# Local attention in 32-query chunks with four heads in 128 rows, value products in four array tiles, and new planner constants, in an attention and expert-MLP kernel on one core

## The chip, the core and the metric

The kernel runs on one core of a Trainium2 chip. The time is device microseconds of one execution, and the comparison uses the median of several runs. The core's engines work in parallel and wait for each other on semaphores: TensorE (PE; its weight loads appear apart, as PEld), VectorE (DVE), ScalarE (ACT), GpSimd (POOL), and SyncE (SP), whose queue issues the transfers from and to device memory.

## What is computed

```python
def _attn_ref(q, k, v):                       # B, H, S, D = 2, 8, 576, 64
    scores = (1 / np.sqrt(D)) * np.matmul(q, k.transpose(0, 1, 3, 2))
    rel = pos[:, None] - pos[None, :]
    mask_local = (rel >= 0) & (rel < 32)                              # heads 0 to 3
    mask_strided = (rel >= 0) & (pos[None, :] % 32 == pos[:, None] % 32)   # heads 4 to 7
    ...                                       # masked softmax
    return np.matmul(attn, v)

def reference(...):
    x = attention laid out as (B * S, H * D)  # 1152 tokens, 512 wide
    x = relu(x @ w_in) ** 2 @ w_out           # d_ff = 2048
    out = sum over e of p[:, e] * (relu(x @ w1[e]) @ w2[e])           # 4 experts, 1024 wide
```

## The kernel before

**Three stages.** Attention is done first and partly beside the first MLP; then come the first MLP and the experts. Every MLP product is three PE products (`mm3`, L788 to L790, and L1328 to L1330 in the experts): operands are split into a high and a low part of a short float32 format, and high by high, high by low and low by high are added up in one PSUM bank.

**The order.** `Plan` (L69) is a small scheduler that runs while the program is built. Each task names the engines that may run it, its cost, a rank, what it comes after, and the buffers that it takes and frees. Whenever an engine is free in the plan, it gets the ready task of the lowest rank. The program is then written out in the plan's order, so each engine's order is fixed by costs and ranks, and a table of constants (L222 to L274) sets the ranks. Where PE has nothing to do in the plan ahead of the first MLP product, `plan.filler` puts a 512-column product on zeros there (L1477).

**A set of attention** (`attend`, L525) goes through these steps: load keys, queries and values; `scores` on PE into a bank S; on DVE the maximum and the subtraction, on ACT the exponential, on DVE the sum and its reciprocal, on POOL or DVE the normalisation; `transposes` on PE into a bank T; a copy to `pt` on ACT or DVE; `values` on PE into a bank X; then the high part and the low part of the result into `xt`, the first MLP's input. A set either gets its mask on PE (a product of the identity with the mask, L426 or L497) or on DVE (L554). With `whole` the exponential is one ACT instruction and the sum one on DVE; without it ACT does one exponential with an accumulated sum per unit (L566).

**Strided sets** (L389) hold 2 or 3 residues of the 32 times 18 positions: 36 or 54 queries by as many keys, 8 units, two heads in the two halves of the 128 rows. There are three sets for each of the two batches. Their 16 value products (L447) go to two tiles of the array, since rows and columns both follow `k`:

```python
nc.tensor.matmul(env["X"][k * D : (k + 1) * D, c : c + n], lhsT=env["v3"][rows, 2 * g + h, :], ...)
```

**Local sets** (L460) hold 128 queries (two of the ten hold 64) in chunks of `WQ` = 64 queries by `WIN` = 96 keys. A unit is one chunk of two heads, one in each half of the 128 rows; a set of 128 queries has 4 units, 8 score products of 64 x 96 (L502), 4 transposes (L506) and 8 value products with 96 rows of keys (L516).

Six sets start before the first MLP product (three strided, three local, `startup`, L601), seven run beside the first steps of the MLP and three beside the next ones. The MLP's first steps read only the first block of 384 tokens.

**Profile names.** `by`, `bh` and `ba` are PSUM banks (four, two and two), `idle` the zeros of the filler, `cb` the constants, `w` split weights, `raw` loaded ones.

## Time and profile before

| | before |
|---|---|
| median of 3 runs | 616.07 us (615.63 to 616.36) |
| span of the profiled execution | 614.7 us |
| PE busy | 608.4 us, 99% of the span, 3737 products |
| DVE busy | 452.9 us, 74% |
| ACT busy | 302.4 us, 49% |
| POOL busy | 125.4 us, 20% |
| read from device memory | 42.13 MB |

The span runs from the first to the last instruction that the profiler recorded; a run's time has some 1.4 us around it. Busy is the union of an engine's rows, and a PE row is longer than the time until the next product starts, because products are pipelined. So PE is read from start to start.

### The profile page before, as it was taken

To read this page: it belongs to the slowest core of one execution; us is meant where nothing else is said; L and a number is where in the kernel's file an instruction comes from. 1 tells how busy PE (TensorE), PEld (TensorE's weight loads), DVE (VectorE), ACT (ScalarE), POOL (GpSimd) and SP (SyncE) were. 2 spreads that over 40 slices of the span, in tenths; PEclk is the share of its full clock that TensorE was granted. 3 is DMA by queue.
4 is the path that set the end of the run, shared out by engine and by line. 5 is a ranking of instruction groups with operands and counts; after the bars stand their busy time and mean duration, and the time that the engine had idled before them with its cause. 6 is when DMAs were issued, how large, how long until landed. Compare 5 with 4: busy or idle time off the path is not lost.

```text
span 614.7 us, 10054 instructions
## 1 busy us (share of the span) xinstructions
PE 608.4 (99%) x3737; PEld 558.4 (91%) x3737; DVE 452.9 (74%) x900; ACT 302.4 (49%) x705; POOL 125.4 (20%) x150
## 2 busy tenths in 40 slices
PE   8999999999999999999999999999999999999997
PEld 5898999999999999998898989898998989898996
DVE  5997958774797984977666675858866776987654
ACT  3676875656464653665244534344344534344330
POOL 2421202310010101032031231312141322224000
PEclk9999999999999999999999999999999999999999
DMA  8987332131213100020110202020201203020012
GB/s 262 315 262 204 110 110 92 34 108 66 102 50 89 36 0 18 1 86 18 38 49 20 84 18 86 18 86 17 71 16 36 70 17 86 18 86 1 1 52 103
DMA packets 37441, 45.14 MB, mean 73 GB/s; under 512 B 4688, under 2 KB 26640, under 8 KB 37392
## 3 DMA queue, kind: packets, MB, share of 16 engines
q1 hardware_dynamic: 37392, 44.50, 23.7%
q8 instruction: 29, 0.48, 0.3%
q14 instruction: 20, 0.16, 0.1%
HBM read 42.13 MB, written 2.36 MB: 72 GB/s over the span
## 4 chain that ended last, share of the span: by engine, by line
PE 97%; DMA 1%; ACT 0%; DVE 0%; SPq 0%; issue 0%; POOL 0%; ACTq 0%
PE bh L788 12%; PE bh L790 12%; PE bh L789 12%; PE by L1329 11%; PE by L1328 11%; PE by L1330 11%; PE by L788 5%; PE by L790 5%; PE by L789 5%; PE ba L788 4%; PE ba L790 4%; PE ba L789 3%; PE ba L516 1%; PE ba L502 1%; DMA q<-in_ql_dram 1%; DMA k<-in_ks_dram 1%
## 5 line engine op out<-in xcount | busy, mean ns | idle before, releaser
L1281 DVE SCALAR_TENSOR_TENSOR acc<-by,pe,acc 128x512 f32<-128x512 f32 (+1 forms) x109 | 79.3, 743 | 24.2 <-PE by L1330 23.9
L788 PE MATMUL bh<-x,w 128*128 128x384 f32 x234 | 80.4, 344 | 0.0
L790 PE MATMUL bh<-x,w 128*128 128x384 f32 x234 | 78.4, 335 | 0.0
L789 PE MATMUL bh<-x,w 128*128 128x384 f32 x234 | 78.4, 335 | 0.0
L1226 POOL TENSOR_TENSOR sf<-raw,raw 128x256 f32<-128x256 f32 x40 | 32.1, 812 | 185.8 <-DMA raw<-in_w_dram 95.9
L1237 ACT ACTIVATE w<-sf 128x256 fp32r<-128x256 f32 x110 | 42.0, 406 | 35.8 <-POOL sf L1226 35.8
L1329 PE MATMUL by<-o,h 128*128 128x512 f32 (+1 forms) x134 | 52.3, 390 | 0.0
L1328 PE MATMUL by<-o,h 128*128 128x512 f32 (+1 forms) x134 | 52.0, 388 | 0.0
L788 PE MATMUL by<-h,w 128*128 128x384 f32 x152 | 51.8, 341 | 0.0
L1330 PE MATMUL by<-o,h 128*128 128x512 f32 (+1 forms) x134 | 51.7, 386 | 0.0
L790 PE MATMUL by<-h,w 128*128 128x384 f32 x152 | 50.8, 334 | 0.0
L789 PE MATMUL by<-h,w 128*128 128x384 f32 x152 | 50.8, 334 | 0.0
L788 PEld LDWEIGHTS bh<-x,w 128*128 128x128 f32 x234 | 43.9, 188 | 2.5 <-DVE r L1448 1.1
L789 PEld LDWEIGHTS bh<-x,w 128*128 128x128 f32 x234 | 44.0, 188 | 0.4
L790 PEld LDWEIGHTS bh<-x,w 128*128 128x128 f32 x234 | 43.9, 188 | 0.0
L1350 ACT ACTIVATE h<-r 128x384 fp32r<-128x384 f32 x26 | 13.7, 525 | 53.6 <-DVE r L1448 53.6
L1226 POOL TENSOR_TENSOR sf<-sf,raw 128x256 f32<-128x256 f32 x40 | 32.2, 815 | 29.1 <-DVE w L1245 29.0
L1448 DVE TENSOR_TENSOR r<-r,bh 128x384 f32<-128x384 f32 x50 | 27.6, 551 | 12.9 <-ACT r L1443 8.3
L789 PE MATMUL bh<-w,w 128*128 128x384 f32 x110 | 36.9, 336 | 0.0
L790 PE MATMUL bh<-w,w 128*128 128x384 f32 x110 | 36.9, 335 | 0.0
L788 PE MATMUL bh<-w,w 128*128 128x384 f32 x110 | 36.8, 335 | 0.0
L1258 ACT ACTIVATE o<-raw 128x512 fp32r<-128x512 f32 x30 | 18.8, 631 | 35.5 <-PE by L1330 35.1
(286 smaller groups left out, 1607.7 us busy)
## 6 DMA issues: line engine op xcount, KB each, us to landing
raw<-in_wi_dram SPq DMA_DIRECT2D x16, 512.0 KB, 3.5
raw<-in_wo_dram SPq DMA_DIRECT2D x16, 512.0 KB, 3.9
raw<-in_w_dram SPq DMA_DIRECT2D x64, 128.0 KB, 2.7
raw<-in_w_dram SPq DMA_DIRECT2D x32, 256.0 KB, 2.8
out_dram<-acc SPq DMA_DIRECT2D x8, 256.0 KB, 2.0
v<-in_vs_dram SPq DMA_DIRECT2D x6, 256.0 KB, 5.1
v<-in_vl_dram SPq DMA_DIRECT2D x8, 192.0 KB, 5.4
k<-in_kl_dram SPq DMA_DIRECT2D x8, 160.0 KB, 4.9
```

The costliest lines, as they stand in the source:

```text
L788: nc.tensor.matmul(dst, lhsT=wh, rhs=xh, start=start, stop=False, skip_group_check=again)
L789: nc.tensor.matmul(dst, lhsT=wh, rhs=xl, start=False, stop=False, skip_group_check=again)
L790: nc.tensor.matmul(dst, lhsT=wl, rhs=xh, start=False, stop=stop, skip_group_check=again)
L1226: nc.gpsimd.tensor_tensor(out=value(dst), in0=value(x), in1=value(y), op=ALU.subtract if n in MINUS else ALU.add)
L1237: nc.scalar.activation(out=op_slot(env["op"])[:, 0].rearrange("p k f -> p (k f)"), in_=value(src), func=AF.Copy, scale=float(sign))
L1258: nc.scalar.activation(out=late[env["w2"]][:, 0], in_=f32(raws[f]["raw"][:, DM:]), func=AF.Copy)
L1281: nc.vector.scalar_tensor_tensor(out=acc, in0=o, scalar=pcol, in1=acc, op0=ALU.mult, op1=ALU.add)
L1328: nc.tensor.matmul(o, lhsT=h[:, 0, ts], rhs=w[:, 0], start=new, stop=False)
L1329: nc.tensor.matmul(o, lhsT=h[:, 0, ts], rhs=w[:, 1], start=False, stop=False)
L1330: nc.tensor.matmul(o, lhsT=h[:, 1, ts], rhs=w[:, 0], start=False, stop=stop)
L1350: nc.scalar.activation(out=got(env["hid"])[:, 0], in_=src(), func=AF.Relu)
L1448: nc.vector.tensor_tensor(out=at_(), in0=at_(), in1=bank["bank"][:, :TB], op=ALU.add if sign > 0 else ALU.subtract)
```

## The change

**Local sets.** A set is now 192 queries in six chunks of 32 queries by 64 keys. A unit is one chunk with all four local heads in the 128 rows, 32 rows each, so a set has 6 units and 24 score products of 32 stationary columns by 64 moving ones, in tiles of 64 rows by 32 columns (two row halves, four column quarters). Two units fill 128 columns of transposed probabilities, so there are 3 transposes. There are 24 value products with 64 rows of keys: the first 64 rows of `pt` belong to the even chunk, the others to the odd one, and each goes to a bank of its own. Six sets take the place of ten.

**Strided value products.** The 16 products are arranged so that four neighbours use the four 64 x 64 tiles of the array: row half `k` and column half `t`. Results of row half 0 go to one bank and those of row half 1 to a second (`env["X", k]`). The score columns are placed so that the transposes deliver this arrangement. The results of every set are read from two banks, in two groups of instructions.

**Loads and constants.** Values are loaded in two transfers per set, one for each half of the rows, without the unused rows; the identity is copied by POOL from `cb` instead of loaded. The planner gets new costs, a cost of 96 ns for changing between tiled and whole-array products, and a new table of ranks, some of which order the weights' conversions and the loads. Five sets come in `startup` (three strided, two local), five in `second`, two in `third`; `ON_PE` and `WHOLE` choose anew which sets are masked on PE and which use one exponential.

```diff
-LOCAL = [[(0, 128), (128, 128), (256, 128), (384, 128), (512, 64)], [(0, 128), (128, 64), (192, 128), (320, 128), (448, 128)]]
-WQ = 64
+NQ_LOCAL = 192
+WQ = 32
 WIN = WQ + STRIDE
...
+    SWITCH = 96
...
-    AHEAD = 10013
-    END2 = 24614
-    END3 = 330
-    CONV = 22941
+    AHEAD = 13732
+    END2 = 22305
+    END3 = 1017
+    CONV = -15359
...
-    CONV1 = 31773
-    CONV2 = -8455
-    FETCH = 252
-    WITH2 = 817
+    CONV1 = -16486
+    CONV2 = -30904
+    FETCH = 40753
+    WITH2 = -2290
...
-    SQ = (0, 23, 0)
-    R_MASK = -916
-    ON_PE = (1, 0, 1, 0, 0, 0, 0, 0, 0, 0)
+    SQ = (0, 23, 1)
+    R_MASK = -2381
+    ON_PE = (1, 1, 0, 0, 0, 0, 0)
...
-    FIRST = (-22394, 16695, 607, 23035, 8563, 1593)
-    WHOLE = (1, 1, 1, 0, 0, 0)
...
+    FIRST = (-13817, -42960, 12541, -38237, -55708)
+    WHOLE = (0, 1, 1, 0, 1, 1, 1, 1, 1, 1, 0, 1)
...
+    LKQ = (-3919, -33009, -13533, -6546, 255)
+    LV = (23587, -34844, 3981, 825, 14657)
+    LW = {('wi', 0, 1): -15243, ('wi', 0, 0): -28071, ('wi', 1, 1): -26551, ('wo', 0, 0): -24768, ('wo', 0, 1): 22478, ('wi', 1, 0): -30156}
+    EARLY = {('wi', 0, 1): 15489, ('wi', 0, 0): -52228, ('wi', 1, 1): 84864, ('wo', 0, 0): -23863, ('wo', 0, 1): -5263, ('wi', 1, 0): -9637}
...
     GROUP = 4
-    AHEAD_H = 3
...
+    AHEAD_H = 1
+    EARLY_H = ((26018, -36435, -4566, -1488), (-17825, 12070, 65861, 27367), (-40517, -11597, 24938, 24933), (66282, -32711, 29856, -6782))
...
-    plan.ring("k", many(at, "k", NQ, [P, U * N3]))
-    plan.ring("v", many(at, "v", NV, [P, 512]))
+    plan.ring("k", many(at, "k", NQ, [P, KCOLS]))
+    plan.ring("v", many(at, "v", NV, [P, VCOLS]))
...
     def mm_r(n):
-        return int(n / 2.4) + 13
+        return 229 if n == 512 else int(n / 2.4) + 13
...
-    t_ci = plan.add({"dma": dma(P * P * 4)}, lambda e: nc.sync.dma_start(out=ident, in_=a["ci"]), rank=L_ID)
+    t_ci = plan.add({"pool": 450}, lambda e: nc.gpsimd.tensor_copy(ident, cb[:, :P]), after=[t_cb], rank=L_ID)
...
-            self.nx = 2 * GROUPS * n
-            self.bytes = [P * U * n * 4, P * U * n * 4, P * U * D * 4]
-            self.cost_s = mm_r(U * n) + 2 * U * packed(n, n) + 100
+            self.nx = GROUPS * n
+            self.bytes = [P * U * n * 4, P * U * n * 4, 2 * n * U * D * 4]
+            self.cost_s = U * (104 if n > 36 else 93)
...
-            self.cost_v = 4 * GROUPS * packed(n, D)
+            self.cost_v = GROUPS * 150
...
-                nc.sync.dma_start(out=env["v"], in_=a["vs"][b, self.j])
+                src = a["vs"][b, self.j].rearrange("(t p) (k c) -> k p t c", t=2, k=2)
+                for k in range(2):
+                    nc.sync.dma_start(out=env["v"][k * D : k * D + n, : U * D].rearrange("p (t c) -> p t c", t=2), in_=src[k, :n])
...
         def values(self, env):
             n = self.n
-            for h in range(2):
-                for g in range(GROUPS):
-                    c, q = (h * GROUPS + g) * n, g * P + h * D
-                    for k in range(2):
-                        rows = slice(k * D, k * D + n)
-                        nc.tensor.matmul(env["X"][k * D : (k + 1) * D, c : c + n], lhsT=env["v3"][rows, 2 * g + h, :], rhs=env["pt"][rows, q : q + n], start=True, stop=True)
...
+            for g in range(2):
+                for h in range(2):
+                    for t in range(2):
+                        c, q = (h * 2 + g) * n, (t * 2 + g) * P + h * D
+                        for k in range(2):
+                            rows = slice(k * D, k * D + n)
+                            nc.tensor.matmul(env["X", k][t * D : (t + 1) * D, c : c + n], lhsT=env["v3"][rows, t, g, h, :], rhs=env["pt"][rows, q : q + n], start=True, stop=True)
...
+        def results(self):
+            parts, m = [], 0
...
+                for x in range(2):
+                    def ends(env, blk=blk, c=c, k=k, m=m, x=x):
+                        src = env["X", x][:, : self.nx].rearrange("p (h r m) -> p h m r", h=2, m=NM)[:, :, m : m + k]
+                        r = self.r0 + 2 * x * self.R
+                        dst = xt[blk][:, :, 2:4, c : c + k * STRIDE].rearrange("p s h (m r) -> p s h m r", r=STRIDE)[:, :, :, :, r : r + 2 * self.R]
+                        return dst, src
...
-            self.t0, self.nq = LOCAL[b][j]
-            self.nj = self.nq // WQ
-            self.units, self.cols, self.pitch = 2 * self.nj, WIN, WIN
-            self.nx = 2 * self.nq
...
+            self.b, self.t0 = b, j * NQ_LOCAL
+            self.nq = NQ_LOCAL
+            self.units, self.cols, self.pitch = self.nq // WQ, WIN, WIN
+            self.nx = self.nq
...
+            self.cost_s = self.units * 120
+            self.pairs = self.units // 2
+            self.cost_t = self.pairs * 109
+            self.cost_v = self.pairs * 180
...
-                nc.sync.dma_start(out=env["v"][:WIN, : 4 * nq], in_=a["vl"][b, :, t0 * 4 : (t0 + nq) * 4])
+                src = a["vl"][b, :, t0 * 8 : (t0 + nq) * 8].rearrange("p (j k c) -> k p j c", k=2, c=4 * D)
+                for k in range(2):
+                    nc.sync.dma_start(out=env["v"][k * D : (k + 1) * D, : 4 * nq].rearrange("p (j c) -> p j c", c=4 * D), in_=src[k])
...
             for u in range(units):
-                j, t = divmod(u, 2)
-                for h in range(2):
-                    hd = slice(h * D, (h + 1) * D)
-                    nc.tensor.matmul(s[hd, u * WIN : (u + 1) * WIN], lhsT=env["q3"][hd, u, :], rhs=env["k3"][hd, t, j * WQ : j * WQ + WIN], start=not masked, stop=not masked or u == units - 1)
+                for t in range(2):
+                    for h in range(2):
+                        hd, r, c = slice(h * D, (h + 1) * D), (2 * h + t) * WQ, u * WIN
+                        nc.tensor.matmul(s[r : r + WQ, c : c + WIN], lhsT=env["q3"][hd, 2 * u + t, :], rhs=env["k3"][hd, t, u * WQ : u * WQ + WIN], start=not masked, stop=not masked or u == units - 1)
...
         def transposes(self, env):
-            for u in range(self.units):
-                nc.tensor.transpose(env["T"][:WIN, u * P : (u + 1) * P], env["p"][:, u * WIN : (u + 1) * WIN], ident)
-
-        def pt_shape(self):
-            return WIN, self.units * P
+            for g in range(self.pairs):
+                cs = slice(g * P, (g + 1) * P)
+                nc.tensor.transpose(env["T"][:, cs], env["p"][:, cs], ident)
...
         def values(self, env):
-            for u in range(self.units):
-                for h in range(2):
-                    j, t = divmod(u, 2)
-                    c = t * self.nq + j * WQ
...
+            for j in range(self.pairs):
+                for t in range(2):
+                    c = (t * self.pairs + j) * WQ
+                    for h in range(2):
+                        for half_ in range(2):
+                            rows, q = slice(half_ * D, (half_ + 1) * D), j * P + (2 * h + t) * WQ
+                            nc.tensor.matmul(env["X", half_][h * D : (h + 1) * D, c : c + WQ], lhsT=env["v3"][rows, j, 2 * t + h, :], rhs=env["pt"][rows, q : q + WQ], start=True, stop=True)
...
-        t = plan.add({"pe": g.cost_t}, lambda e: g.transposes(env), after=[t, t_ci], rank=rank + r_t, take=[(env, "T", rings)], free=[(env, "p")])
+        t = plan.add({"pe": g.cost_t}, lambda e: g.transposes(env), after=[t, t_ci], rank=rank + r_t, take=[(env, "T", rings), (env, "pt", ["pt"])], free=[(env, "p")])
...
-        t_v = plan.add({"pe": g.cost_v}, lambda e: g.values(env), after=[t, loads[2]], rank=rank + r_v, take=[(env, "X", rings)], free=[(env, "pt"), (env, "v")])
+        t_v = plan.add({"pe": g.cost_v}, lambda e: g.values(env), after=[t, loads[2]], rank=rank + r_v, take=[(env, ("X", k), rings) for k in range(2)], free=[(env, "pt"), (env, "v")], tiled=True)
...
-    startup = [Strided(0, j) for j in range(3)] + [Local(0, j) for j in range(3)]
+    startup = [Strided(0, j) for j in range(3)] + [Local(0, j) for j in range(2)]
...
-    second = [Local(0, 3), Local(0, 4)] + [Strided(1, j) for j in range(3)] + [Local(1, 0), Local(1, 1)]
+    second = [Local(0, 2)] + [Strided(1, j) for j in range(3)] + [Local(1, 0)]
     for k, g in enumerate(second):
-        attend(g, START - AHEAD + k * (due(half) - START - END2) // len(second), ["bank_a"], LEAD, whole=g.units > 4, on_pe_=ON_PE[k])
-    third = [Local(1, j) for j in (2, 3, 4)]
+        attend(g, START - AHEAD + k * (due(half) - START - END2) // len(second), ["bank_a"], LEAD, whole=WHOLE[5 + k], on_pe_=ON_PE[k])
+    third = [Local(1, j) for j in (1, 2)]
...
+        attend(g, due(half) - AHEAD + k * (due(2 * half) - due(half) - END3) // len(third), ["bank_a"], LEAD, whole=WHOLE[10 + k], on_pe_=ON_PE[len(second) + k])
```

**Ahead of the first MLP product, on PE.** Here is what stands between two fillers in the middle of the startup, before; `k`, `q` are a set's keys and queries, `p` probabilities, `pt` transposed ones.

```order
L497 LDWEIGHTS cb
L497 MATMUL ba_105<-cb 128x384
L502 MATMUL ba_105<-k_115,q_111 64x96 x8
L447 MATMUL by_108<-pt_130,v_119 64x54 x16
L435 MATMUL ba_106<-ident,p_127 128x128 x4
L497 LDWEIGHTS cb
L497 MATMUL by_109<-cb 128x384
L502 MATMUL by_109<-k_116,q_112 64x96 x8
```

And now, with rows of further products of the same kind left out at the dots:

```order
L444 MATMUL by_107<-cb 128x432
L450 MATMUL by_107<-k_118,q_114 54x54 x16
L465 MATMUL ba_106<-pt_129,v_119 64x54
L465 MATMUL by_108<-pt_129,v_119 64x54
...
L455 MATMUL by_109<-ident,p_125 128x128 x4
L1506 LDWEIGHTS idle
L1506 MATMUL by_110<-idle 128x512
...
L520 LDWEIGHTS cb
L520 MATMUL ba_105<-cb 128x384
L525 MATMUL ba_105<-k_115,q_111 32x64 x24
L530 MATMUL ba_106<-ident,p_126 128x128 x3
```

A value set's products now alternate between two banks; a local set has 24 score products and 3 transposes; the third local score set (`by_109<-k_116`) has moved behind the first MLP products, and fillers stand at places where attention stood.

**Up to the first MLP product, on PE**, before (`bh_103<-x_75,w_80` is that product):

```order
L447 MATMUL ba_105<-pt_130,v_122 64x36 x16
L506 MATMUL by_107<-ident,p_129 96x128 x4
L506 MATMUL ba_106<-ident,p_128 96x128 x4
L1477 LDWEIGHTS idle
L1477 MATMUL by_110<-idle 128x512
...
L788 MATMUL bh_103<-x_75,w_80 128x384
```

And now:

```order
L530 MATMUL ba_106<-ident,p_128 128x128 x3
L465 MATMUL ba_105<-pt_130,v_123 64x54
L465 MATMUL by_107<-pt_130,v_123 64x54
...
L1506 MATMUL by_110<-idle 128x512
L539 MATMUL ba_106<-pt_129,v_122 64x32
L539 MATMUL by_109<-pt_129,v_122 64x32
...
L817 MATMUL bh_103<-x_75,w_80 128x384
```

Before, no local value product stood ahead of the first MLP product; now those of both startup sets do, with five fillers between the last of them and that product. In all 53 fillers stand there, where there were 23.

**On SP**, the first transfers, before and now:

```order
L365 DMA cb<-in_cb_dram 128x410
L413 DMA k_115<-in_ks_dram 128x432
L415 DMA q_111<-in_qs_dram 128x432
L413 DMA k_116<-in_ks_dram 128x432
L415 DMA q_112<-in_qs_dram 128x432
L417 DMA v_119<-in_vs_dram 128x512
```

```order
L435 DMA v_119<-in_vs_dram 54x2x256 x2
L429 DMA k_115<-in_ks_dram 128x432
L431 DMA q_111<-in_qs_dram 128x432
L382 DMA cb<-in_cb_dram 128x346
L762 DMA raw_90<-in_wi_dram 128x1024
L429 DMA k_116<-in_ks_dram 128x288
```

The first values (two transfers) have moved ahead of the first keys, and the constants behind the first queries; a load of first-layer weights now stands fifth in the list.

## Rows read from the trace of the kernel before

**Rows 1.** The page: busy time by engine, and the chain's shares by engine.
```profile
PE 608.4 (99%) x3737; PEld 558.4 (91%) x3737; DVE 452.9 (74%) x900; ACT 302.4 (49%) x705; POOL 125.4 (20%) x150
PE 97%; DMA 1%; ACT 0%; DVE 0%; SPq 0%; issue 0%; POOL 0%; ACTq 0%
```

**Rows 2.** Timeline of PE to the first MLP product: start, length in us, instructions.
```profile
0.98 4.02 PE L1477 MATMUL by<-idle 128*128 128x512 bf16 x9 [0.98 <-DVE idle L1481]
4.80 0.57 PE L426 MATMUL ba<-cb 128*128 128x432 bf16 x1
...
6.55 0.36 PE L426 MATMUL ba<-cb 128*128 128x432 bf16 x1
...
9.43 1.47 PE L1477 MATMUL by<-idle 128*128 128x512 bf16 x6
10.74 0.33 PE L497 MATMUL ba<-cb 128*128 128x192 bf16 x2
...
14.69 0.88 PE L502 MATMUL ba<-k,q 64*64 64x96 f32 x16
...
20.53 0.64 PE L506 MATMUL by<-ident,p 128*96 128x128 f32 x4 [0.29 <-POOL p L576]
...
21.75 0.52 PE L788 MATMUL bh<-x,w 128*128 128x384 f32 x1
```

**Rows 3.** Timeline of PE behind it; x16 are the records of 8 products.
```profile
23.70 0.34 PE L497 MATMUL ba<-cb 128*128 128x384 bf16 x1
23.97 0.88 PE L502 MATMUL ba<-k,q 64*64 64x96 f32 x16
24.78 0.44 PE L788 MATMUL bh<-x,w 128*128 128x384 f32 x1
25.06 0.34 PE L789 MATMUL bh<-x,w 128*128 128x384 f32 x1
...
25.41 0.60 PE L506 MATMUL by<-ident,p 128*96 128x128 f32 x4
25.76 0.42 PE L788 MATMUL bh<-x,w 128*128 128x384 f32 x1
26.02 0.34 PE L789 MATMUL bh<-x,w 128*128 128x384 f32 x1
26.20 0.34 PE L790 MATMUL bh<-x,w 128*128 128x384 f32 x1
26.47 0.69 PE L516 MATMUL ba<-pt,v 96*64 96x64 f32 x16
27.14 0.69 PE L516 MATMUL by<-pt,v 96*64 96x64 f32 x16
27.76 0.44 PE L788 MATMUL by<-x,w 128*128 128x384 f32 x1
...
29.48 0.36 PE L426 MATMUL ba<-cb 128*128 128x432 bf16 x1
29.77 1.01 PE L430 MATMUL ba<-k,q 64*54 64x54 f32 x32
30.71 0.45 PE L788 MATMUL bh<-x,w 128*128 128x384 f32 x1
...
39.44 0.75 PE L430 MATMUL ba<-k,q 64*36 64x36 f32 x32
40.12 0.44 PE L788 MATMUL by<-h,w 128*128 128x384 f32 x1
```

**Rows 4.** Chain that ended last: start, time to the next piece, what.
```profile
46.29 1.07 PE ba L447 x32
```

**Rows 5.** Windows: stretch, its length, PE, PEld, DVE, ACT, POOL busy.
```profile
40.00:50.00 10.00, 9.90 (x131) 8.86 (x125) 9.53 (x28) 7.02 (x16) 1.83 (x2) 1.00 0.55 164
```

**Rows 6.** PE's waits: total us, times, longest.
```profile
PE ba L430 <- DMA q<-in_qs_dram: 0.6, 2, 0.4
```

**Rows 7.** Groups of PE instructions to 100 us by form: busy us, mean ns.
```profile
L430 PE MATMUL ba<-k,q 64*36 64x36 f32 x64 | 1.5, 200 | 0.2 <-DMA q<-in_qs_dram 0.2
```

## The prediction

> **What bounds the kernel now.** I read the page first. TensorE (PE) is busy 99% of the span and carries 97% of the chain that ended last [rows 1], so the time is what PE has to issue plus what it waits for. Next I read PE's timeline. The first product of the first MLP layer starts at 21.75 us [rows 2]. After it PE issues without a gap worth naming, up to a short tail that the change doesn't touch. The waits list agrees: apart from the first microsecond, the longest wait of a product is 0.4 us, for a transfer, and the longest stand ahead of the first MLP product [rows 6]. VectorE (DVE) is nearly full only around there (9.53 of 10 us in 40 to 50 us, [rows 5]). So two numbers set the time: when the first product starts, and how much attention work PE still has to do after it. Both are read from start to start of PE's rows, not from their lengths, because a row's length holds a tail that overlaps the next row.

> **The paces that the sum uses.** A float32 attention product leaves two records. The rows show two tiles of the array working side by side: the 36-column strided scores leave 32 records in 0.75 us, the last of them 0.20 us long [rows 3, 7], so (0.75 - 0.20)/31 = 17.7 ns per record, or 35 ns per step of two. A 54-column set takes 29.77 to 30.71 = 0.94 us and a 36-column set 39.44 to 40.12 = 0.68 us, both 16 steps [rows 3]: 0.26/(16 x 18) = 0.9 ns per column and step. A 96-column local set takes 23.97 to 24.78 = 0.81 us for 8 steps [rows 3], about 80 ns a step and 0.17 us of drain. A 64-column step lies between: 60 ns from the strided line. For the value products, 16 steps take 1.07 us [rows 4] and 8 steps take 27.14 to 27.76 = 0.62 us [rows 3]: 56 ns a step, and I use 58 ns and 0.15 us of drain. Their stationary side is 64 columns in both, and stays so. Four transposes cost 25.41 to 25.76 = 0.35 us, and a mask product 23.70 to 23.97 = 0.27 (local) or 29.48 to 29.77 = 0.29 us (strided) [rows 3]. Going from whole-array products into tiled ones costs 0.1 us (26.20 to 26.47 against a plain pitch of 0.17), and coming back costs 0.1 us (24.78 to 25.06; after transposes 25.76 to 26.02) [rows 3].

> **First part: the new sets on PE.** A local set now covers 192 queries. It has 24 score products in tiles at two row and four column places, which is 48 records; four at a time that is 12 steps of 60 ns and 0.14 us of drain, 0.85 us. It has 3 transposes where the 6 units of the same queries had 6. It has 24 value products, 48 records: four at a time 12 x 58 ns + 0.15 = 0.85 us. A strided value set keeps its 16 products, but in four tiles: 8 steps, 0.62 us where it was 1.07. No row of before shows four tiles at once. It shows two pairs: scores on different rows and columns, local values on all rows with different columns. The nearest bounds are therefore four at a time (above) and two at a time: 24 steps and 1.55 us for a local set's scores or values, 1.07 us for strided values. I take four, since each pair alone runs without a loss per step, and the second bank takes away the one place that two row halves would share.

> **Second part: PE's work behind the first product.** Before, counted from the program's order: 5 full and 2 half local score sets (5 x 0.81 + 2 x 0.49 = 5.0), masks 0.56, strided scores 2 x 0.94 + 0.68 = 2.56, 40 transposes 3.5, local values 8 x 0.62 + 2 x 0.38 = 5.7, strided values 3 x 1.07 = 3.2; together 20.6 us. There are 14 entries and 23 returns, 3.7 us. After, from the new order: 4 local score sets 3.4, masks 0.56, strided scores 2.56, 24 transposes 2.1, local values 4 x 0.85 = 3.4, strided values 3 x 0.62 = 1.9; together 13.9 us. There are 13 entries and 20 returns, 3.3 us. The difference is **-7.1 us**.

> **Third part: the first product starts later.** The new order puts both local sets of the first block completely ahead of it and has 53 filler products where 23 stood. Summed: PE starts at 0.98 [rows 2]; ten early fillers at (4.80 - 0.98)/9 = 0.424 us bring it to 5.2; the first score set as before, 4.80 to 6.55 [rows 2], to 7.0; 43 later fillers at (10.74 - 9.43)/6 = 0.218 us [rows 2] are 9.4; a strided score set of 36 columns 0.9 and one of 54 columns 1.2; two local ones 2 x (0.27 + 0.85) and an extra mask piece, 2.3; 18 transposes at 0.11, 2.0; strided values 3 x 0.62; local values 2 x 0.85. The sum is 26.3 us, that is **+4.55 us** if nothing waits longer than the fillers cover. The strictest wait is the second local set. Its scores end near 18.5 us in this sum and its transposes are due near 23.2, 4.7 us later, with maximum, subtraction, exponential, sum and normalisation in between. Before, a local set took 14.69 to 20.53 = 5.8 us from its scores to its transposes [rows 2], though with eight small ScalarE instructions in it that this set no longer has. So x lies between 26.3 and 27.4; I take 26.3. It isn't earlier, since fillers are in the program whether needed or not.

> **Edits costed at nothing.** On SyncE's queue the first strided values (two halves) now stand ahead of the first keys, queries and constants; they delay the first scores by about 0.7 us, and the tenth early filler covers most of that. The identity is made by GpSimd from the constants instead of a transfer; it is due at the first transposes, some 8 us later. If that cover failed, the whole start would move by the same amount. DVE loses work (a third of the local columns and half of the copies of transposed probabilities) and gains small result copies, since each set now ends in two banks; the fillers and the 0.5 us around 40 us where it is full stay the limits. The planner's numbers reorder the rest; from the 1,113th MLP product on PE's order is the same as before, and no wait there was long.

> **Sum.** -7.1 + 4.55 = -2.55 us on the profiled execution, whose span is 1.4 us under the median of the runs; carried over to the median: 616.07 - 2.55 = **613.5 us**, 0.4% faster. About 0.2% is what a measurement of this kernel can tell from no change.

> **The rivals.** *Issue limits the four tiles.* If a record can't be issued faster than the 17.7 ns that rows show, a local set's 48 records take 0.85 us instead of 0.70, twice in 6 sets, and 32 strided ones 0.57 instead of 0.47, in 6 sets: +2.4 us, 615.9, no difference to be told. For it: no row is faster on average. Against it: within a step the second record follows the first closely, and the pace falls with the columns, so columns set it. Chance 0.15.
> *The tiles don't run four at a time* (the slower side). Place: all 12 local score and value sets and 6 strided value sets. Price: 0.7 us for each of the 12, 0.45 for each of the 6, +11.1 us, 624.6, +1.4%. It decides as soon as more than 2.5 us of that is lost, under a quarter. A milder form holds every record to the mean pace of the 54-column set, (0.94 - 0.12)/32 = 25.6 ns [rows 3]: 0.5 us more in each of the 12 and 0.35 in the 6, +8.1, 621.6. Against it stand the 36-column records, one every 17.7 ns [rows 3, 7]. Chance of the two forms 0.13. [...]
> *The start waits longer than its fillers.* The 5.8 us of before hold for the second local set too: x at 27.4, 614.6; with the late landing of values 615.3. Chance 0.10.
> *The reordered middle stalls.* Weight conversions were moved far down in rank, so a weight tile could come late between 40 and 220 us, in some tenths each: 616 to 618. Against it: DVE has less to do up to each of these points. Chance 0.07.

> **How the numbers follow.** The forecast has 0.55, from 612.4 (a shorter drain) to 614.9. Faster: 0.52 of it, half of the late start and a little else, 0.57. No difference: the issue limit, the other half and part of the stalls, 0.27. Slower: 0.16. The range runs from 612.3 to 618.0; it leaves out the two forms of missing concurrency (0.13) and about 0.05 at the ends.

> **What would show it.** In the profile after: 24 local score products from first to last start in about 0.7 us, a strided value set in 0.47; the first product at 26 to 27 us; no PE gap over 0.3 us behind it. If local sets need 1.4 us, the second rival holds; if PE shows waits ahead of the last transposes, the third. Wrong altogether: PE waits behind the first product that add up to over 2 us.

## The result: slower, 620.4 us

| | before | after |
|---|---|---|
| median | 616.06 us (615.63 to 616.36, 4 runs) | 620.44 us (620.25 to 621.49, 4 runs) |
| ratio after to before, 95% interval | | 1.0075 [1.0061, 1.009] |
| span of the profiled execution | 614.7 us | 619.7 us |
| PE products | 3737 | 4036 |
| first product of the first MLP layer starts at | 21.75 us | 33.49 us |
| from it to the end | 592.9 us | 586.2 us |

The forecast was 613.5 us, with 618.0 as the upper end. The changed kernel is 4.4 us slower than before. The last two lines of the table show the form of it. The part behind the first MLP product became shorter, about as forecast (-6.7 us, forecast -7.1), though by luck: two misses nearly cancel in it, as the sum below shows. The start became 11.7 us longer, where 4.55 had been forecast. The profile of after is that of the slowest of its four executions (621.49 us, mean granted clock 0.994), and the others, one of them at 0.999 and 620.61 us, left none, so the shares of the stop and of the half clock below hold for that one execution.

The page of after, which answers [rows 1]: PE's busy time, and the shares of the chain that ended last, by engine.

```profile
PE 610.5 (99%) x4036; PEld 555.1 (90%) x4036; DVE 446.6 (72%) x885; ACT 303.9 (49%) x696; POOL 126.1 (20%) x150
PE 97%; issue 1%; DMA 1%; ACT 0%; DVE 0%; SPq 0%
```

A share of 1% has appeared for "issue", time in which PE waited for nothing that the profile shows. The waits of PE say where (after; total us, times, longest), against [rows 6]:

```profile
PE ba L539 <- issue: 3.3, 1, 3.3
PE by L1506 <- DVE idle L1510: 1.0, 1, 1.0
PE ba L444 <- DMA cb<-in_cb_dram: 0.9, 1, 0.9
PE by L465 <- ACT mid L768: 0.5, 1, 0.5
```

The timeline of PE in after (start, length, instructions) shows the places, against [rows 2]:

```profile
6.31 0.36 PE L444 MATMUL ba<-cb 128*128 128x432 bf16 x1 [0.88 <-DMA cb<-in_cb_dram]
...
25.14 0.31 PE L539 MATMUL ba<-pt,v 64*64 64x32 f32 x1 [3.33 <-issue]
...
25.71 2.32 PE L1506 MATMUL by<-idle 128*128 128x512 bf16 x5
27.82 1.06 PE L455 MATMUL ba<-ident,p 128*128 128x128 f32 x4
28.67 1.88 PE L1506 MATMUL by<-idle 128*128 128x512 bf16 x5
...
33.49 0.52 PE L817 MATMUL bh<-x,w 128*128 128x384 f32 x1
```

Three things are to be seen. The first strided scores start 1.1 us later than in my sum, since they wait for the constants. PE stands still from 21.6 to 25.14 us in the middle of the first local value set (L539): 18 of its 24 products are done, and the other 6 use the same tiles and need nothing new. And what follows the stop runs at half speed: five fillers take 2.1 us, 0.42 us each, against 0.218 in my sum, and four transposes 0.85 (27.82 to 28.67) against 0.35 [rows 3].

The windows of after (stretch, its length, PE, PEld, DVE, ACT, POOL, PE's granted clock, DMA share, GB/s):

```profile
22.00:23.00 1.00, 0.00 (x0) 0.00 (x0) 0.00 (x0) 0.00 (x0) 0.75 (x1) 1.00 0.99 175
23.00:24.00 1.00, 0.00 (x0) 0.00 (x0) 0.00 (x0) 0.00 (x0) 0.00 (x0) 0.56 0.95 277
24.00:29.00 5.00, 3.86 (x22) 2.27 (x23) 3.19 (x13) 1.01 (x4) 0.83 (x1) 0.50 0.72 165
30.00:31.00 1.00, 1.00 (x18) 0.64 (x20) 0.01 (x1) 0.08 (x1) 0.00 (x0) 1.00 0.49 94
```

The granted clock fell from 1.00 to 0.50 during the stop and came back shortly before 30 us (0.52 in 29 to 30), five microseconds after PE had taken up work again. No engine but POOL does anything in 22 to 24 us; what DVE and ACT do next, at 25.81 and 25.85 us, waits for PE's local values (L539).

**What PE waited for.** No semaphore stands at the stop. The trace's DMA records show a transfer on the queue of kind instruction, which I read as a piece of the program itself. The DMA view of after for 22.1 to 23.7 us (queue: packets, MB, share of 16 engines' time):

```profile
q8 instruction: 1, 0.02, 5.8%
```

One packet of 16 KB took 5.8% of 16 x 1.6 us, 1.5 us: by its record it ran from 22.15 to 23.65 us. PE went on at 25.14, 1.5 us after it had landed. After has 4036 products and as many weight loads and 31 such packets, about 260 PE instructions to a packet. Counting PE's recorded instructions (products, weight loads and those of its sequencer), the stop falls between number 705 and number 706. In the kernel before the corresponding packet ran at nearly the same time, 22.05 to 23.28 us, but PE reached instruction 705 only at 26.6 us, 3.3 us after the landing. If PE needs the 1.5 us from landing to start there too, it had about 2 us to spare; in after it was there 5 us earlier (21.6 us), with more and shorter instructions ahead of that point.

**The sum, measured.** By the profiled executions (619.7 against 614.7 us of span; the forecast was 2.55 below 614.7):

| stretch | forecast | measured | miss |
|---|---|---|---|
| to the first MLP product | 26.3 us | 33.49 us | +7.2 |
| first to 1,113th MLP product (210.1 us, before 218.3) | -7.1 | -8.2 | -1.1 |
| 1,113th MLP product to the end (376.2 us, before 374.6) | 0 | +1.5 | +1.5 |

The start's 7.2 us are, but for 0.2, made of 1.1 up to the last strided values of 36 columns (the wait for the constants, and 0.5 for ACT), 3.5 of the stop, and 2.4 of the half clock behind it (25.14 to 33.49 us is 8.35; the same rows of my sum are 5.95, and in e9 and e11 below, where the clock stayed at 1.00, they take 6.06).

### The profile page after: what moved, and what is told of

Read it like the earlier page. It is cut to its first block, busy times and chain, and to the rows that moved or that the text cites. A ratio compares the mean times of both kernels' runs of the same rounds, so it can differ in the third digit from the quotient of the medians.

```text
span 619.7 us, 10605 instructions
## 1 busy us (share of the span) xinstructions
PE 610.5 (99%) x4036; PEld 555.1 (90%) x4036; DVE 446.6 (72%) x885; ACT 303.9 (49%) x696; POOL 126.1 (20%) x150
## 4 chain that ended last, share of the span: by engine, by line
PE 97%; issue 1%; DMA 1%; ACT 0%; DVE 0%; SPq 0%
PE bh L817 12%; PE bh L818 12%; PE bh L819 12%; PE by L1358 11%; PE by L1359 11%; PE by L1357 11%; PE by L817 5%; PE by L818 5%; PE by L819 5%; PE ba L818 3%; PE ba L817 3%; PE ba L819 3%; PE by L1506 2%; PE ba L539 1%; PE ba L450 1%
## 5 line engine op out<-in xcount | busy, mean ns | idle before, releaser
L1290 DVE TENSOR_TENSOR o<-raw,o 128x512 fp32r<-128x512 f32 x30 | 21.1, 706 | 21.9 <-ACT o L1287 21.9
L793 POOL TENSOR_TENSOR w<-val,w 128x512 fp32r<-128x512 f32 x13 | 17.6, 1357 | 91.8 <-ACT w L787 44.7
L1477 DVE TENSOR_TENSOR r<-r,bh 128x384 f32<-128x384 f32 x50 | 27.5, 551 | 12.0 <-ACT r L1472 7.8
```

The source lines that it names most:

```text
L1290: nc.vector.tensor_tensor(out=late[env["w2"]][:, 1], in0=f32(raws[f]["raw"][:, DM:]), in1=f32(late[env["w2"]][:, 0]), op=ALU.subtract)
L1477: nc.vector.tensor_tensor(out=at_(), in0=at_(), in1=bank["bank"][:, :TB], op=ALU.add if sign > 0 else ALU.subtract)
```

## The experiments

The theory from the profile of after: instruction blocks come too late for a program of short products, and the half clock follows from the stop. Rivals: it is the place in the kernel (the bank, the value tile, a semaphore that the profile does not show) or the crowded transfer engines.

### e1, e2: move the block's edge

```diff
+    SPLIT = {n: 4 for n in range(20, 24)}          # e1; in e2 range(33)
...
     def warm(e):
-        nc.tensor.matmul(spare, lhsT=idle, rhs=spread(idle, 4), start=True, stop=True)
+        for c in range(0, 512, 512 // k):
+            nc.tensor.matmul(spare[:, c : c + 512 // k], lhsT=idle, rhs=idle[:, : 512 // k], start=True, stop=True)
```

> The kernel after, with four of its fillers (the first four of the nine behind the first local scores) issued as four products of 128 columns each: the same columns, 24 more instructions on PE. In the profile of after PE stands still for 3.3 us behind 36 of the 48 records of the first local value set (21.6 to 25.1 us). Theory A (PE's program itself came late: PE counts 8,118 instructions and the page 31 transfers of 16 KB on the queue of kind instruction, 262 per transfer; the block with the next instructions wasn't there): the stop stands 24 instructions, that is 12 records, earlier in the program, behind 24 of the 48 records (give or take 2), and is about as long, 3 to 4 us; time 620 to 621. Theory B (the stop belongs to these products, their operands or banks): it stays behind record 36. Theory C (something that happens at 21.6 us on the clock): it stays there on the clock, so at record 36 or within 0.2 us of it, also when the fillers take a little longer.

> The kernel after, with the first 33 of its 53 fillers issued as four products of 128 columns each: the same columns, 198 more instructions on PE ahead of the stop. Theory A: the limit of the block moves 198 instructions back in the program, to where the second local scores start (about 18.3 us), and the block before it is begun at about 11.4 us, so PE has 6.9 us for the transfer where it had 3.8; the next limit falls behind the second local set's transposes. The stop goes or shrinks to under 1 us; the first MLP product starts at 26.5 to 28.5 us (33.5 in after) and the time is 613 to 616. Theories B and C: the stop stays, 3 us or more, at the same products or the same time; 620 to 621.5.

e1: 619.87 us (619.07 to 620.67), ratio 1.0064 [1.0044, 1.0084]. e2: 619.76 (618.65 to 622.08), 1.0067 [1.0045, 1.009]. The timeline of PE in e1:

```profile
17.55 0.26 PE L465 MATMUL by<-pt,v 54*64 54x54 f32 x1 [1.47 <-issue]
...
23.70 0.24 PE L539 MATMUL ba<-pt,v 64*64 64x32 f32 x1 [1.11 <-issue]
```

With 24 instructions more ahead of it, the stop stands again behind PE's instruction 705, which is now 24 instructions earlier in the set; another stands behind instruction 449, 256 earlier. At both the blocks had landed 1.4 us before PE went on (16.16 and 22.34 us). In e2 the 705th instruction lies in another set, in the local scores, and the stop has gone there (0.9 us, 20.55 to 21.69 from start to start). The waits of PE in e2:

```profile
PE ba L444 <- DMA cb<-in_cb_dram: 1.8, 1, 1.8
...
PE ba L525 <- issue: 1.2, 2, 0.9
```

So the stop belongs to the count of instructions, not to a tile, a bank or a product. Theory A had the place right in both runs; the lengths in e1 and the time of e2 it had wrong. The totals stay near 620 in both: e1 has two shorter stops, and e2 waits 1.8 us for the constants, with the clock at 0.57 in 8 to 12 us. What a stop costs is also seen in e1: with stops of 1.1 and 1.5 us the clock stays at 1.00 and the first MLP product starts at 29.89 us, 3.6 earlier than in after.

### e3: the kernel before with 150 instructions more

```diff
+    SPLIT = {n: 8 if n < 3 else 4 for n in range(21)}      # in the kernel before; warm as in e1
```

> The kernel before, with nothing of its attention changed: 21 of its 23 fillers are issued as four (three of them as eight) products of fewer columns, the same columns in all, 150 more instructions. Theory A: the limit that PE passed at 26.8 us moves to the last transposes ahead of the first MLP product, which PE reaches at 20.5 us. If the block's transfer starts as late as in before (22.05 us, 1.2 us long), PE stands there for 2 to 4 us and the time is 618 to 621; if it starts earlier by as much as its block is begun earlier (15.0 for 18.0 us), the stop is 0 to 1.5 us and the time 616 to 618. Theories B and C: no stop, first MLP product at 21.7 to 22.2 us, 616.0 to 616.6.

617.75 us (615.6 to 619.62), 1.0028 [1.0013, 1.0042]. No issue stop appeared in its profile. What it has is a wait for queries (e3, waits of PE), with the clock at 0.68 in 12 to 16 us:

```profile
PE ba L502 <- DMA q<-in_ql_dram: 1.9, 1, 1.9
```

So this run does not show that instructions alone bring the stop into the kernel before. It is inconclusive for the block, and it shows a second thing: with PE's early work in more and shorter products, PE waited 1.9 us for these queries where before waits 0.4, and the mean clock behind that wait was 0.68 (12 to 16 us) and 0.90 (16 to 20 us).

### e4: one transfer for the local values

```diff
-                for k in range(2):
-                    nc.sync.dma_start(out=env["v"][k * D : (k + 1) * D, : 4 * nq].rearrange("p (j c) -> p j c", c=4 * D), in_=src[k])
+                nc.sync.dma_start(out=env["v"][:, : 4 * nq], in_=a["vl"][b, t0 // NQ_LOCAL])
```

> The kernel after, with the local values laid out in device memory as the 128 rows read them, so that each set is one transfer of 3 KB per row where there were two of 64 rows with 1 KB pieces; the same bytes, PE's program unchanged. Theory A with the load on the transfer queues as what holds the block up: the 1 KB pieces that stand ahead of it are moved faster, its transfer starts 0.5 to 2 us earlier than at 22.15 us, the stop at record 36 shrinks from 3.3 to 1.5 to 3 us, time 618 to 620. Theory A without the load (the block is only asked for late): the stop stays 3.2 to 3.5 us, 620 to 621. Theory B, if it is a wait for the values of this set: the stop goes, since one early transfer brings them; C: unchanged.

620.04 us (616.38 to 622.27), 1.0057 [1.0037, 1.0077]. The stop is there again, 2.45 us long, and the windows of e4 show what follows:

```profile
24.00:28.00 4.00, 4.00 (x13) 2.07 (x13) 3.98 (x14) 1.59 (x4) 0.83 (x1) 0.50 0.02 7
```

The transfer engines are at 0.02 here, and the clock is at 0.50 all the same, so the slow products after this stop came with the half clock and not with busy transfers. Whether crowded engines make the block late is not settled. With the lighter load the block of the stop came earlier (20.85 to 21.91 us, against 22.15 to 23.65) and the stop was 0.9 us shorter, which is what the expectation gave for the load; the time was hardly better. Against the load as the whole reason stands the next block: PE went over the edge at 23.45 us, and its transfer began only at 30.82, though the engines were at 0.02 from 24 to 28 us. Why it begins so late stays open.

### e5: value products ordered for two tiles at a time

```diff
-                    for h in range(2):
-                        for half_ in range(2):
+            for half_ in range(2):
+                for j in range(self.pairs):
```

> The kernel after with the value products in another order, all of one row half first and then all of the other: the same products, banks and instructions, but neighbours are in two tiles of the array and not in four. If the tiles work four at a time in after, a local value set's 48 records take 1.3 to 1.5 us to the last start for 0.73 to 0.78, and a strided set's 32 about 0.95 for 0.5; four local and three strided sets behind the first product cost some 4 us more. The stop at the 705th recorded PE instruction stays; it may be 0.5 us shorter, since PE comes there later. Time 622 to 626. If the four tiles were no faster than two, the time is that of after, 620 to 621.5.

624.27 us (624.1 to 624.44), 1.0137 [1.0119, 1.0154]. This tests the second rival of the prediction. First the timeline of PE in after: a local score set, a local value set, a strided value set of 54 columns, each with the row behind it.

```profile
35.51 0.87 PE L525 MATMUL ba<-k,q 64*32 64x64 f32 x48
36.31 0.44 PE L817 MATMUL bh<-x,w 128*128 128x384 f32 x1
...
43.40 0.90 PE L539 MATMUL ba<-pt,v 64*64 64x32 f32 x48
44.23 0.45 PE L817 MATMUL bh<-x,w 128*128 128x384 f32 x1
...
51.09 0.69 PE L465 MATMUL ba<-pt,v 54*64 54x54 f32 x32
51.71 0.44 PE L817 MATMUL by<-h,w 128*128 128x384 f32 x1
```

From start to start they take 0.80, 0.83 and 0.62 us; forecast were 0.85, 0.85 and 0.62, in four tiles. The same places in e5:

```profile
43.80 1.39 PE L539 MATMUL ba<-pt,v 64*64 64x32 f32 x48
45.12 0.45 PE L817 MATMUL bh<-x,w 128*128 128x384 f32 x1
...
51.98 0.96 PE L465 MATMUL ba<-pt,v 54*64 54x54 f32 x32
52.87 0.44 PE L817 MATMUL by<-h,w 128*128 128x384 f32 x1
```

1.32 and 0.89: without neighbours on the other row half a set costs 0.49 and 0.27 us more. Four local and three strided value sets stand behind the first MLP product, 4 x 0.49 + 3 x 0.27 = 2.8 us; the stretch from it to the 1,113th MLP product grew by 2.5 (212.6 against 210.1 us). The value products of the change run four at a time, at the pace that I had taken. The price of two at a time was too high in the rival, 0.70 and 0.45 us.

### h1, h2: the start of before, the new sets behind it

```diff
     startup = [Strided(0, j) for j in range(3)] + [Local(0, j) for j in range(3)]
-    second = [Local(0, 3), Local(0, 4)] + [Strided(1, j) for j in range(3)] + [Local(1, 0), Local(1, 1)]
+    second = [Local2(0, 2)] + [Strided4(1, j) for j in range(3)] + [Local2(1, 0)]      # h2: Strided(1, j)
-    third = [Local(1, j) for j in (2, 3, 4)]
+    third = [Local2(1, j) for j in (1, 2)]
```

`Local2` and `Strided4` are the sets of the change; the planner keeps before's table of ranks. In h1 the strided values are loaded into the wrong halves of the rows, so those sets multiply other numbers; the instructions are the same.

> The six sets of attention that start ahead of the first MLP product are those of before, with its order, its 23 fillers and its constants; only the sets behind them have the new form (four local sets of 192 queries, three strided ones with values in four tiles), their local values loaded in one transfer. Theory A (the change's gain behind the first product is real; its loss is the start, where PE's instructions came late): no stop of PE in the start, first MLP product at 21.7 to 22.0 us as in before; behind it, by rows of after and before, local sets cost 4 x (0.80 + 0.25 + 0.83) = 7.5 us for 11.0, strided values 1.9 for 3.2, and three sets fewer save some 0.5 us of changes: 5 us less, time 610.5 to 612. Theory B (the new sets cost time wherever they stand, by waits of the later engines or by late instructions there too): 614 to 618.

> The same as the kernel with the old start and the new sets behind it, but its three later strided sets keep the values of before (two tiles, one bank). If four tiles give what the rows of after show (0.49 us to the last start of a strided value set for 0.95 in before), this kernel is 1.0 to 1.5 us slower than its fellow: 611.7 to 613.2. If the four tiles give nothing on the path, the two agree within 0.3 us.

h1: 620.4 us (620.16 to 623.33), 1.0082 [1.0067, 1.0097]. h2: 615.41 (614.89 to 616.9), 0.9992 [0.9984, 1.0001]. Both start the first MLP product with before, at 21.73 and 21.49 us. What PE saves behind it they lose there. The waits of PE in h1:

```profile
PE bh L948 <- DVE h L1026: 3.3, 4, 1.3
PE ba L644 <- DVE p L694: 2.4, 3, 1.6
```

and in h2:

```profile
PE ba L457 <- POOL p L716: 1.8, 2, 1.2
...
PE bh L948 <- DVE h L1026: 0.8, 1, 0.8
PE bh L950 <- DVE w L924: 0.4, 1, 0.4
```

DVE is the engine that is full here, 9.49 of 10 us in 40 to 50 us of h2, as it was before [rows 5]. h1 lost in the clock too, 0.83 in the same stretch (windows of h1):

```profile
40.00:50.00 10.00, 8.18 (x108) 7.53 (x109) 7.73 (x24) 3.54 (x10) 2.85 (x3) 0.83 0.58 177
```

Both expectations were missed: h1 was to take 610.5 to 612 us and h2 about 1 us more, and h2 came out 5 us faster than h1. After has no such wait behind its first MLP product, so I infer that its new table, which orders DVE's work anew, belongs to the gain. That isn't shown by itself: after also has other sets ahead of the first MLP product, and its table alone was not tried.

### e6 to e9: repair the start, piece by piece

The pieces: ten of the late fillers moved ahead of the strided values of 36 columns, so that PE does not arrive early (e6); e4's transfer, the same move, the last six fillers left out, and the second local set's sum on DVE ahead of the first set's copies (e7); e7 with constants, keys and queries first on SP and 60 instructions more from ten split fillers (e8); after with only that order on SP (e9).

```diff
+        moved = fill[37:47]                                    # e6, e7, e8
+        q = [x for x in q if x not in moved]
+        k = q.index(fill[36]) + 1
+        q[k:k] = moved
...
+        head = [dmas[3], dmas[1], dmas[2], dmas[0]]            # e8, e9: constants, keys, queries, values
+        q[k:k] = head
```

> The kernel after with ten of its fillers, the two groups of five that stand behind the first local values, moved ahead of the 36-column strided values in front of them; nothing added or taken away. PE comes to the block's limit (the 705th recorded PE instruction, now behind some 26 of the 48 records of the first local values) 2.2 us later, so the block has that much more time. Theory A: the stop shrinks from 3.3 us to between 0 and 1.8 us, the granted clock stays at or near 1.00 in 20 to 30 us (0.66 in after), the first MLP product starts at 28.5 to 31 us and the time is 615.5 to 618.5. Theory B (the stop belongs to these products or to what they wait for) or a block that is only asked for when PE runs dry: the stop stays 3 us or more, and the time is that of after or longer, 620 to 622.

> The kernel after with the ten fillers moved ahead, the local values of a set in one transfer, the last six fillers in front of the first MLP product left out, and on DVE the sum and the reciprocal of the second local set in front of the first copy of the first local set's results. If what after lost is the late block, the halved clock behind it and DVE's queue held up by it, PE has no stop over 1 us in the start, the clock is at 1.00, the first MLP product starts at 26.3 to 28.5 us (33.5 in after) and the time is 613.3 to 616. If something else costs the time behind the start, it stays over 617 though the start is earlier.

> The kernel with the repaired start (ten fillers ahead of the strided values, local values in one transfer, the last six fillers left out, the second local set's sum in front of the first set's copies on DVE), and two edits more: the constants, keys and queries of the first set stand in front of its values on the transfer queue, and the first ten fillers, which run while PE waits for data anyway, are issued as four products of 128 columns each (60 more instructions). Theory A: without the 1.4 us wait for the constants PE starts its scores at 4.8 to 5.6 us as before did and its clock stays full; the block's limit falls at the front of the first local values, some 8 us behind the limit before it where it was 5.9, so PE has no stop over 0.5 us. First MLP product at 25.5 to 27.5 us, time 612.3 to 615. If the stop comes back at the 705th recorded PE instruction though it has 8 us, the time is 615 to 618.

> The kernel after with one edit: on the transfer queue the constants, keys and queries of the first set stand in front of its values. PE's first scores start at 4.8 to 5.6 us (6.31 in after, behind 0.9 us of idle). If the start's wait is a loss of its own, the time is 0.7 to 2 us under after: 618 to 620; the stop at the 705th recorded PE instruction is still there, since all of PE comes earlier by the same amount. If the wait is hidden by the stop (the block comes when it comes), the time stays at 620 to 621.5.

| | median | ratio | first MLP product | longest waits of PE in the start |
|---|---|---|---|---|
| e6 | 621.98 (620.93 to 624.39) | 1.0104 [1.0086, 1.0123] | 34.53 us | POOL 1.3, constants 1.3 |
| e7 | 617.56 (615.68 to 620.38 in 11 runs; a twelfth took 1543.36) | 1.0025 [1.0012, 1.0037] | 30.63 us | constants 1.4, issue 1.2 |
| e8 | 618.13 (617.3 to 620.08) | 1.003 [1.0017, 1.0042] | 29.86 us | queries 2.0, POOL 0.9 |
| e9 | 617.71 (616.71 to 621.52) | 1.0039 [1.0021, 1.0057] | 28.11 us | issue 1.7, queries 1.1 |

None of the four came out at its expected time. e6 is a miss: the stop is all but gone (behind instruction 705 PE goes on after 0.3 us, from start to start), but PE now waits 1.3 us for POOL ahead of the second local set and 1.3 for the constants, and the clock is at 0.76 in 28 to 32 us; the sum is no better than after. e7 and e8 gained 2 to 3 us and show the waits taking turns: in e7 the stop is 1.2 us, in e8 there is none. In e8 a load of raw weights stands on the queue ahead of the queries that PE waits for (waits of PE in e8):

```profile
PE ba L464 <- DMA q<-in_qs_dram: 2.0, 1, 2.0
```

In e10 below, which moves that load back, this wait is gone. e9 is the cleanest of the four, one edit: the first scores start at 5.00 us in place of 6.60, and the stop behind instruction 705 is there with half its length. The waits of PE in e9, and the window with the stop:

```profile
PE ba L545 <- issue: 1.7, 1, 1.7
PE ba L456 <- DMA q<-in_qs_dram: 1.1, 1, 1.1
```

```profile
20.00:24.00 4.00, 2.26 (x42) 1.55 (x35) 1.89 (x11) 1.34 (x4) 0.91 (x1) 1.00 1.07 250
```

Its clock stays at 1.00. A stand of 1.7 us was not followed by a lower clock here; 1.9 in e3 was followed by 0.68, 2.4 in e4 and 3.3 in after by 0.50. In e7 a clock of 0.50 in 28 to 32 us followed a stop of only 1.2 with smaller gaps around it, so in these profiles the length of one stand alone does not tell it. With the clock whole, the first MLP product comes 5.4 us earlier than in after, and the median is 2.7 us lower: the SP order that I had put at nothing has a price. Not all of the 5.4 need be the order's, since e11 below, with the order of after, comes to 28.46 us in its profile.

### e10: the whole start in order

```diff
+        head = [dmas[k] for k in (3, 1, 2, 5, 6, 0, 4)]        # constants, keys, queries twice; values; raw weights
+        q = q[:k] + head + [x for x in q[k:] if x not in head and x not in late and x not in fill[48:]]
```

with e4's transfer, ten early fillers split, the last five left out, and e7's order on DVE.

> The kernel after with its start put right in one place after the other and its attention unchanged: constants, the first two sets' keys and queries in front of the first values and of the first weights on the transfer queue; local values of a set in one transfer; the first ten fillers as four products of 128 columns each (60 more instructions, so that PE's block limit falls at the front of the first local values); the second local set's sum in front of the first set's copies on DVE; the last five fillers left out. Theory A with the three losses named so far (late block, late landing of the first constants and keys, DVE's queue held by the first local values): PE has no wait over 0.7 us up to the first MLP product, the clock stays 1.00, the first MLP product starts at 24.3 to 26.5 us (28.1 in the kernel with the constants first, 33.5 in after) and the time is 612.5 to 615. If it starts that early and the time is 616 or more, something behind the start takes the gain back (weights that come later, DVE): then PE shows waits of 1 us and more behind it.

615.23 us (614.75 to 619.93, 12 runs), 1.0004 [0.9983, 1.0024]. There is no issue stop, and the first product of the MLP starts at 26.82 us (timeline of PE in e10):

```profile
26.82 0.45 PE L826 MATMUL bh<-x,w 128*128 128x384 f32 x1
```

PE still waits for queries, where at most 0.7 us had been expected (waits of PE in e10); its clock is at 1.00 all the same.

```profile
PE ba L534 <- DMA q<-in_ql_dram: 1.4, 1, 1.4
...
PE ba L464 <- POOL p L614: 0.8, 1, 0.8
```

At the 1,113th MLP product e10 is 2.84 us ahead of before, at the 1,901st 2.23, at the last one 1.11. The forecast of 613.5 still isn't reached, although its start and its savings are there. All nine kernels built on the change lose between the first and the last of these points, e10 1.73 us, and of those built on the kernel before (e3, h1, h2) none does, with the same order on PE.

### e11, e12, e13: where the tiles lie

The changed kernel's tile of constants is 346 bf16 columns wide, before's 410. The difference is 128 bytes in each partition, and the tiles that follow it from the same side of the memory, among them those of the MLP and the experts, lie that much lower. h1 and h2, with a second tile of constants of 128 columns, had them 256 bytes higher than before.

```diff
-    cb = const.tile([P, CB], BF16, name="cb")
+    cb = const.tile([P, 410], BF16, name="cb")                 # e11: after; e12: e10
-    ... nc.sync.dma_start(out=cb, in_=a["cb"]) ...
+    ... nc.sync.dma_start(out=cb[:, :CB], in_=a["cb"]) ...
```

```diff
+    cb = const.tile([P, CB + 64], BF16, name="cb")             # e13: before, tiles 128 bytes up
```

> The changed kernel with one edit: the tile of constants is kept 410 columns wide, as in the kernel before, and only its first 346 columns are loaded and used. Every tile behind it then lies at its address of before; without the edit all of them lie 128 bytes lower in each partition. No instruction is added, removed or moved. Theory placement: the loss in the experts' part (from MLP product 1112 to the end the kernel before is 1.75 us faster at the same order on TensorE) comes from the addresses and goes: the second output products of the experts come back from about 235 to about 232 ns from start to start, and the time is near 618.7 us. Rival: something else that all kernels built on the change share (the program's own place, the instruction blocks' phase) makes it: the products stay at 235 ns and the time near 620.4 us.

> e10_start_in_order with the same edit (the tile of constants 410 columns wide, 346 loaded). Theory placement: e10 was 2.84 us ahead of the kernel before at MLP product 1112 and 1.86 at product 1900; with the addresses of before it keeps some 2.8 us to the end: near 613.4 us, ratio about 0.996 to the kernel before. Rival: the drift stays, near 615.2 us, as e10.

> The kernel before with one edit: the tile of constants is kept 474 columns wide in place of 410, of which 410 are loaded and used, so that every tile behind it lies 128 bytes higher in each partition; no instruction is added, removed or moved. In e11 the tiles lay 128 bytes higher than in the changed kernel and the loss in the experts' part was gone; in h2 they lay 256 bytes above the kernel before, with no loss. Theory: what counts is the place modulo 256 bytes (here 32, as in the changed kernel, where before, e11 and h2 have 160); then the kernel before with the tiles 128 bytes up loses some 1.5 to 1.8 us, near 617.7 us, with the second output products of the experts at 235 ns from start to start in place of 232. Rival: only the move downward, or something that the changed kernel's start does, costs it: 616.0 us as before.

| | median | ratio | 1,113th MLP product to the end |
|---|---|---|---|
| e11 | 616.77 (614.39 to 621.09) | 1.0023 [1.0002, 1.0043] | 374.0 us (after 376.2) |
| e12 | 612.33 (612.09 to 615.53) | 0.9954 [0.9938, 0.997] | 373.9 us (e10 376.0) |
| e13 | 618.98 (618.71 to 620.43) | 1.0048 [1.0031, 1.0064] | 377.2 us (before 374.6) |

The groups of PE instructions by form in 250 to 600 us, the third of the experts' output products (busy us, mean ns of one): before,

```profile
L1330 PE MATMUL by<-o,h 128*128 128x512 f32 x122 | 47.5, 389 | 0.0
```

after,

```profile
L1359 PE MATMUL by<-o,h 128*128 128x512 f32 x120 | 47.4, 395 | 0.0
```

e11, the changed kernel with its tiles where before has them,

```profile
L1359 PE MATMUL by<-o,h 128*128 128x512 f32 x122 | 47.5, 389 | 0.0
```

and e13, the kernel before with its tiles 128 bytes up:

```profile
L1330 PE MATMUL by<-o,h 128*128 128x512 f32 x120 | 47.5, 396 | 0.0
```

From start to start, the three products of such a step take 229, 232 and 226 ns (medians) in before and e11, and 231, 235 and 232 in e13. By the means each third of the step is 3.2, 1.8 and 5.7 ns longer in after than in e11; 285 of each stand behind the 1,113th product, 3.0 us, and the 384-column products there give 0.8 back: 2.2 us. The place of the tiles makes it, in either kernel, with no instruction changed. One step of 128 bytes cost 2.2 us down (after against e11) and 2.5 up (e13 against before); h2, two steps up, took 615.41 us in all, 0.9992 of before. e13's loss, 3.2 us by the median, is larger than I expected of it (1.5 to 1.8): 2.5 of its profile's 3.9 lie behind the 1,113th product, 1.3 ahead of it, where the clock was 0.59 in 20 to 24 us. e11's median fell by 3.7 us, more than the 2.2 of the experts. In its profile the stop behind instruction 705 is 1.2 us long, the clock stays at 1.00, the first MLP product comes at 28.46 us, and another stop of 1.0 us stands behind instruction 1,729, at 53 us. Its instructions are those of after, so the length of the stop is not given by them alone. Which tile of the many it is that must not be moved was not tried.

e12 is faster than both kernels, by 0.46% than before and by 1.3% than after. The timeline of PE in e12:

```profile
26.14 0.44 PE L826 MATMUL bh<-x,w 128*128 128x384 f32 x1
```

The forecast had 26.3 us for that product and 613.5 for the whole; e12 has 26.14 and 612.33. It is not the start of the forecast: five fillers (1.1 us) are left out, and PE waits 1.0 us in all.

## Why the prediction was wrong, step by step

**Paces and first part: right.** Four tiles at a time were forecast and ran so (0.80, 0.83, 0.62 us a set against 0.85, 0.85, 0.62). The rival of the missing concurrency is refuted by after's rows, and e5 shows its price. That of the issue limit fell too: from the first to the last start of a strided set's 32 records are 0.47 us, 15 ns a record, under the 17.7 that I took from [rows 3, 7].

**Second part: right in mechanism, 1.1 us too small.** -8.2 us up to the 1,113th product, forecast -7.1. I did not trace the rest. h1 and h2 show what the step did not say: their saving on PE went into its waits for DVE and POOL (3.3 and 2.4 us for DVE in h1; 1.8 for POOL and 0.8 for DVE in h2).

**Third part: failed, at its condition.** The sum of 26.3 us held "if nothing waits longer than the fillers cover". The rows of that sum are about as long as it says (e12 comes to 26.14, with 1.1 us of fillers fewer and 1.0 us of waits). What I looked for were waits for data, and I named the second local set's transposes as the strictest. What waited, by the count of instructions in e1 and e2, was PE for its own program: a stop of 3.3 us, with the half clock behind it, in a start that came to 33.49 us. The 53 fillers did not cover that: they are instructions of it themselves, and with their loads bring the edge of a block sooner (198 instructions more in e2 moved it into the local scores). The row that would have warned me was in the profile of before: the instruction queue's 29 packets, one for some 260 instructions, each 0.9 to 1.4 us long. I should have set the number of instructions to each point of the start against the times at which those blocks arrived: 705 at 26.6 us before, with its block landed at 23.3; and my own sum had PE there at about 20.5 (the 21.6 of after, less the 1.1 us by which it was late).

**Edits costed at nothing: wrong for SP's order.** I put the first values' place ahead of the constants at 0.7 us, covered by the tenth filler. PE waited 0.88 us on top of it, and the median of e9, with the order put back, is 2.7 us lower: the early delay changed which wait came next (0.9 us for the constants and a stop of 3.3 in after; 1.1 for queries and a stop of 1.7 in e9).

**"From the 1,113th MLP product on PE's order is the same as before": right, but the time put at nothing there was +1.5 us.** The same order was not the same time with the tiles moved: 376.2 us in after, 374.0 in e11. A narrower tile of constants is in the diff; I read it as a smaller transfer.

**Rivals.** "The start waits longer than its fillers" (0.10) was the right place with the wrong mechanism, and I priced it at 1.1 us where it cost 7.2. "The middle stalls" did not happen.

**Open.** What the three executions of after without a profile lost, the one at a clock of 0.999 above all. Why the stop behind the same instructions is 3.3 us long in after and 1.2 in e11. Why a block's transfer begins late: it began 5.5 us after PE had entered the block ahead in after, 7.4 in e4 with the transfer engines idle, and 1.4 to 2.6 for the first four blocks of e12. The runs show no rule for it.

## What to carry to other kernels

When an edit trades few long products for many short ones, count instructions as well as time: set the count to each point of a loaded start against the arrival of the instruction blocks in the trace, because the stop of 3.3 us here had no semaphore, and 53 fillers did not hide it. A first delay, even of a microsecond, was worth repairing at its source (0.9 us for the constants in after; with the constants first on the queue, e9 is 2.7 us faster by the median), since in this start it decided what was late next. And when a tile changes its size, compare a version with the old addresses before blaming the instructions: here 128 bytes were 2.2 us.
